# Attention into a Mish feed-forward on one core: where the seventh head pair is scaled and transposed, and four blocks of the first product computed before their Mish

## The chip, the core and the metric

One core of one Trainium2 chip runs the whole program. The engines are TensorE (PE, with its weight loads PEld), VectorE (DVE), ScalarE (ACT), GpSimd (POOL) and SyncE (SP), which here only issues DMAs. The metric is the device time of one execution in microseconds (us), lower is better. All times without a unit below are in us; places in the profile are in us from the start of the profiled span.

## The reference

Attention over 8 batches of 12 heads, 448 positions of 64 values, with one added to the softmax's sum (in the form exp(-m)), and then a feed-forward with Mish between two products.

```python
    scale = 1.0 / np.sqrt(q.shape[-1])
    scores = scale * np.matmul(q, k.transpose(0, 1, 3, 2))
    m = np.max(scores, axis=-1, keepdims=True)
    e = np.exp(scores - m)
    attn = e / (np.sum(e, axis=-1, keepdims=True) + np.exp(-m) + 1e-09)
    return np.matmul(attn, v).astype(np.float32)
...
    x = np.ascontiguousarray(attn_out.transpose(0, 2, 1, 3)).reshape(B * S, H * D)
...
    h = x @ w_in
    sp = np.where(h > 20.0, h, np.log1p(np.exp(np.minimum(h, 20.0))))
    g = h * np.tanh(sp)
    return (g @ w_out).astype(np.float32)
```

`w_in` is 768 x 2048 and `w_out` 2048 x 768. Inputs and output are float32; the kernel multiplies in bf16.

## The kernel before

The order of the instructions on every engine is written out by hand; nothing reorders them, and each engine works through its own list, waiting where data or a buffer is missing.

**Pairs, units, parts.** Two heads make a pair, six pairs a batch, 48 pairs in all. Pairs 0 to 5 are done one by one in a lead (the loop at L548). From pair 6 on three pairs make a unit, `u` = 2 to 15 (L575), and two more units finish the feed-forward. A unit has an exp part, 12 steps `n` (four per pair), and a Mish part, eight blocks `f`. In the Mish part of unit `u` the first product of the batch before is computed: units 2 and 3 do blocks 0 to 7 and 8 to 15 of batch 0. From unit 4 on the exp part also holds the second product (`w_out`) as filler.

**A pair's way.** SP loads q, k and v (`load_pair`), POOL casts them (`cast_pair`, L162 to L176), PE transposes q and k (L193), DVE and ACT copy them out of PSUM (`evac_qk`). PE computes the scores of two tiles at a time, up to three steps ahead (`scores_ahead`, three PSUM tiles `sc`), DVE takes their negated maximum (L293), ACT the exponentials with their sums (L306). `denominators` (L318) makes the reciprocals on DVE; `normalise` (L325) scales the seven tiles of `en` on DVE (L341) or POOL (L339, from a copy `rden2` of the reciprocals). The scaled tile is transposed into `eT` either by one DMA transpose on SP's queue (L345) or, for the pairs in `BY_PE`, in four parts by PE into an `mo` bank with a copy by DVE (`turn_on_pe`, L356 and L360). `av_pair` (L382) multiplies with v, and the result is cast into `xT`, the transposed input of the feed-forward (L391).

**Buffers.** There are two `mo` banks in PSUM, handed out in turn; an entry in `late` holds a copy out of one, made at the next `flush_late`. `eT` has three buffers, `en` four (`en_bufs[p % 4]`), `o_sb` four. Each DMA on SP's queue also waits until the eighth before it has landed.

**Around the change.** Unit 2 makes pairs 6, 7 and 8. At the start of its Mish part the reciprocals of all three are made at once; DVE scales pair 8 (DMA transpose), DVE scales pair 6 at block 3, and POOL scales pair 7 at block 4. Pairs 6 and 7 are turned by PE in unit 3's exp part, at the steps of `TURN_AT[1]` (L521); the value products follow at the steps of `AV_AT` (L530): pair 6 at step 5, pair 7 at 8, pair 8 at 10. The pieces of `w_in` and `w_out` are loaded by POOL's DMA queue at the steps of `W_AT` (L532) and at L629; pieces 6 to 8 of `w_in` hold blocks 8 to 11, pieces 9 to 11 blocks 12 to 15. `mm1_mish` (L399) computes one block of six matmuls, into an `mo` bank or, for block 1 of a unit, into a spare `sc` tile, and ACT applies Mish from PSUM (L412); ACT loads the table for Mish at the part's start and that for Exp at its end (L649). From pair 12 on two of three q tiles have a block-diagonal form, whose zero halves DVE writes once (L223, L224) before pairs 13 and 14.

Of the kernel before, what the change touches and what calls it, by code (L numbers as in the profile page):

```python
# [19 lines left out]
def kernel(  # L20
# [21 lines left out]
    UNITS_PER_B = HP // UNIT_PAIRS  # L42
    N_UNITS = B * UNITS_PER_B
# [157 lines left out]
    def evac_qk(p, act=False):  # L201
# [6 lines left out]
        if not is_diag(p):  # L208
            qT = qd.rearrange("d i h r -> d (i h r)")[:, 0:S]
            qkT[p] = (qT, kT)  # L210
            if act:
                nc.scalar.mul(qT, q_ps[:, 0:S], SCALE)
            else:
                nc.vector.tensor_scalar(
                    out=qT, in0=q_ps[:, 0:S], scalar1=SCALE, scalar2=None, op0=ALU.mult
                )
            if p >= DIAG_FROM:
                nc.gpsimd.tensor_copy(out=q_rest[0:64, 0, :], in_=qT[0:64, 384:S])
                nc.gpsimd.tensor_copy(out=q_rest[64:128, 1, :], in_=qT[64:128, 0:64])
        else:  # L220
            qkT[p] = (qd, kT)
            if p < DIAG_FROM + 3:
                nc.vector.memset(qd[0:64, :, 1, :], 0.0)  # L223
                nc.vector.memset(qd[64:128, :, 0, :], 0.0)  # L224
            for h in range(2):
                rows = slice(64 * h, 64 * h + 64)
                nc.vector.tensor_scalar(  # L227
                    out=qd[rows, :, h, :],
                    in0=q_ps[rows, 0:S].rearrange("d (i r) -> d i r", i=QB),
                    scalar1=SCALE, scalar2=None, op0=ALU.mult,  # L230
                )
# [66 lines left out]
    def exps(idx):  # L298
# [13 lines left out]
        if s == STEPS - 1 and p < HP:  # L312
# [11 lines left out]

    def normalise(p, dma=True, on_pool=False, shared=0):  # L325
        st = att[p]
        en = st["en"]
        if on_pool or shared:

            st["rden2"] = st_pool.tile([128, NTILE], FP32, tag="rden2", name="rden2")  # L330
            nc.vector.tensor_copy(out=st["rden2"], in_=st["rden"])  # L331
        for i in range(NTILE):
# [66 lines left out]
    def mm1_mish(b, ff):  # L399
        if ff == 0:  # L400
            gT[b] = gT_pool.tile([128, FF_T, S], BF16, tag="gT", name="gT")
        flush_late()
        spare = ff % FF_U == 1
        h_ps = sc_tiles[0][:, 0, :] if spare else mo_take()
        for dm in range(DM_T):
# [5 lines left out]
            )  # L411
        nc.scalar.activation(out=gT[b][:, ff, :], in_=h_ps[:, 0:S], func=AF.Mish)  # L412
# [80 lines left out]
    for g in range(B // 2):  # L493
# [12 lines left out]
        else:  # L506
# [9 lines left out]
    HEAD = HP  # L516

    BY_PE = (2, 4, HEAD - 1, HEAD, HEAD + 1)
    TURN_AT = (
        {0: [(4, 2)], 1: [(4, 3)], **{3 + j: [(HEAD - 1, j)] for j in range(NT)}},  # L520
        {0: [(HEAD, 0), (HEAD, 1)], 1: [(HEAD, 2)], 2: [(HEAD, 3)],  # L521
         3: [(HEAD + 1, 0)], 4: [(HEAD + 1, 1)], 5: [(HEAD + 1, 2)], 6: [(HEAD + 1, 3)]},
    )
# [6 lines left out]
    AV_AT = ({3: 4, 7: 3, 9: 5}, {5: 6, 8: 7, 10: 8})  # L530

    W_AT = ({5: 1, 9: 1}, {1: 1, 4: 1, 5: 1, 7: 1, 9: 1, 11: 1}, {3: 1, 5: 1, 7: 1, 9: 1})  # L532
# [42 lines left out]
    for u in range(UNITS_PER_B, N_UNITS + 2 * UNITS_PER_B):  # L575
# [10 lines left out]
        for n in range(steps):  # L586
# [8 lines left out]
            if u == UNITS_PER_B + 1:  # L595
                for part in TURN_AT[1].get(n, []):
                    turn_on_pe(*part)
            flush_late()
# [22 lines left out]

# [3 lines left out]
        todo = sorted(range(p0, nxt), key=lambda p: p in BY_PE)  # L625
        for f in range(FF_U):
            if moe:
                mm1_mish(b, w * FF_U + f)
            if u == UNITS_PER_B and f in (2, 6):  # L629
# [13 lines left out]
            if f == 3:  # L643
# [40 lines left out]
```

## Time and profile before

| | us |
|---|---|
| median of 3 runs (lowest to highest) | 481.56 (480.86 to 481.75) |
| the profiled execution | 479.95 |
| its span, first to last instruction | 478.0 |
| PE busy | 443.1 (93%) |
| DVE / ACT / POOL busy | 339.1 / 350.0 / 181.1 |
| mean granted TensorE clock | 0.982 |

Busy time is that in which an engine has an instruction in work; matmuls overlap, so a busy PE isn't at its peak. The granted clock is the share of full speed that TensorE was given. In a timeline row the first number is the start, the second the length, and what stands in brackets is the idle time before it and what ended it; several equal instructions are merged (x7). SPq rows are DMA issues on SP's queue; the time from issue to landing is given apart. The page's costliest groups (line, engine, operation, count, busy time and mean ns of one, idle time before) include:

```profile
L306 ACT ACTIVATE en<-sc,negm 128x448 bf16<-128x448 f32 x336 | 209.6, 637 | 26.4 <-DVE xT L391 10.4
L412 ACT ACTIVATE gT<-mo 128x448 bf16<-128x448 f32 x112 | 61.3, 547 | 68.2 <-PE mo L406 68.1
L339 POOL TENSOR_SCALAR en<-en,rden 128x448 bf16<-128x448 bf16 x122 | 76.4, 646 | 80.7 <-DVE rden L331 76.9
L341 DVE TENSOR_SCALAR en<-en,rden 128x448 bf16<-128x448 bf16 x214 | 58.6, 345 | 0.9
L459 DVE COPY o_sb<-mo 128x384 f32<-128x384 f32 (+1 forms) x65 | 32.2, 495 | 35.1 <-PE mo L472 34.8
```

Unit 2 runs from about 48 to 76.75, unit 3 to 104.29 (exp part to 92.17), and from unit 4 on a unit takes about 26.

### The profile page before, as it was taken

Reading aid. Unit: us, or ns where it says so; the run is one execution under the profiler, and the core shown is the slowest. Engines: PE = TensorE matmul, PEld = TensorE weight load, DVE = VectorE, ACT = ScalarE, POOL = GpSimd, SP = SyncE. Lnnn points to the kernel's source line nnn. Section 1 sums busy time; section 2 is a strip of 40 time slices with the busy share of each in tenths; the row PEclk is TensorE's granted clock in tenths of the full one; section 3 lists DMA queues with packets and bytes.
Section 4 is the critical chain, followed back from the end, with each engine's and each line's share of the span. In section 5 each row is a group of like instructions: output and inputs, shape, how many; then the busy total and the mean of one; then the engine's idle time right before and its main releaser. Section 6 shows DMA issues by size and latency. Waiting matters only on the chain.

```text
span 478.0 us, 8924 instructions
## 1 busy us (share of the span) xinstructions
PE 443.1 (93%) x3064; PEld 248.6 (52%) x3064; DVE 339.1 (71%) x680; ACT 350.0 (73%) x919; POOL 181.1 (38%) x315
## 2 busy tenths in 40 slices
PE   4565888898999999999999999999999999999997
PEld 2233544454655555555555555556555555556565
DVE  4888987968787886878687878788787869420021
ACT  5979678878787888979787878888897978412300
POOL 4877809255514334353535242433535340300000
PEclk9998798899999999999999999999999999999999
DMA  8999969999999989899999999899989595870113
GB/s 228 220 233 220 235 100 234 162 187 238 207 217 276 206 212 219 213 203 246 193 250 182 225 167 228 211 207 234 201 233 212 156 178 127 135 164 24 43 28 105
DMA packets 202381, 90.37 MB, mean 189 GB/s; under 512 B 159072, under 2 KB 198880, under 8 KB 202336
## 3 DMA queue, kind: packets, MB, share of 16 engines
q1 hardware_dynamic: 194848, 83.51, 81.3%
q0 software_dynamic: 7488, 6.29, 8.6%
q8 instruction: 24, 0.39, 0.3%
q14 instruction: 21, 0.17, 0.1%
HBM read 45.61 MB, written 11.01 MB: 118 GB/s over the span
## 4 chain that ended last, share of the span: by engine, by line
PE 76%; ACT 10%; DVE 9%; issue 2%; DMA 1%; POOL 0%; SPq 0%; DVEq 0%; ACTq 0%; POOLq 0%
PE mo L472 26%; PE mo L406 25%; ACT en L306 9%; PE sc L382 6%; DVE negm L293 6%; PE sc L266 5%; PE sc L406 4%; PE sc L193 3%; PE sc L272 2%; PE mo L356 1%; PE mo L382 1%; DVE en L341 1%; PE sc L280 1%; DVE eT L360 1%; DMA k_f<-in_k_dram 1%
## 5 line engine op out<-in xcount | busy, mean ns | idle before, releaser
L306 ACT ACTIVATE en<-sc,negm 128x448 bf16<-128x448 f32 x336 | 209.6, 637 | 26.4 <-DVE xT L391 10.4
L293 DVE TENSOR_REDUCE negm<-sc 128x2 f32<-128x896 f32 x192 | 180.7, 968 | 55.8 <-PE sc L275 26.0
L472 PE MATMUL mo<-w_out_sb,gT 128*128 128x384 bf16 (+1 forms) x912 | 142.3, 301 | 0.0
L406 PE MATMUL mo<-xT,w_in_sb 128*128 128x448 bf16 x672 | 137.7, 353 | 0.6 <-DVE xT L391 0.6
L412 ACT ACTIVATE gT<-mo 128x448 bf16<-128x448 f32 x112 | 61.3, 547 | 68.2 <-PE mo L406 68.1
L472 PEld LDWEIGHTS <-gT 128*128 128x128 bf16 x912 | 84.1, 98 | 48.2 <-issue 5.7
L339 POOL TENSOR_SCALAR en<-en,rden 128x448 bf16<-128x448 bf16 x122 | 76.4, 646 | 80.7 <-DVE rden L331 76.9
L406 PEld LDWEIGHTS <-w_in_sb 128*128 128x128 bf16 x768 | 72.9, 98 | 64.0 <-issue 3.0
L306 ACT ACTIVATION_READ_ACCUMULATOR en<-sc,negm 128x1 f32 x336 | 69.3, 206 | 0.0
L175 POOL CAST q_bf<-q_f 112x512 bf16<-112x512 f32 x47 | 29.0, 617 | 98.4 <-DMA q_f<-in_q_dram 98.0
L341 DVE TENSOR_SCALAR en<-en,rden 128x448 bf16<-128x448 bf16 x214 | 58.6, 345 | 0.9
L459 DVE COPY o_sb<-mo 128x384 f32<-128x384 f32 (+1 forms) x65 | 32.2, 495 | 35.1 <-PE mo L472 34.8
L266 PE MATMUL sc<-kT,qd 128*128 128x448 bf16 x168 | 47.7, 354 | 0.3 <-ACT en L306 0.2
L272 PE MATMUL sc<-kT,qd 64*128 64x448 bf16 x72 | 25.1, 411 | 12.7 <-ACT en L306 11.1
L382 PE MATMUL sc<-eT,v_bf 112*64 112x448 bf16 x288 | 34.1, 357 | 1.9 <-ACT en L306 1.7
L162 POOL CAST v_bf<-v_f 112x512 bf16<-112x512 f32 x48 | 29.5, 616 | 9.7 <-DMA v_f<-in_v_dram 8.8
L382 PEld LDWEIGHTS <-v_bf 112*64 112x64 bf16 x384 | 21.0, 112 | 22.8 <-issue 13.6
L176 POOL CAST k_bf<-k_f 112x512 bf16<-112x512 f32 x47 | 28.9, 616 | 7.5 <-DMA k_f<-in_k_dram 7.0
L227 DVE TENSOR_SCALAR qd<-sc 64x448 bf16<-64x448 bf16 x48 | 18.7, 389 | 11.9 <-PE sc L193 11.2
L266 PEld LDWEIGHTS <-qd 128*128 128x128 bf16 x168 | 16.3, 97 | 18.0 <-issue 9.2
L275 PE MATMUL sc<-kT,qd 64*128 64x448 bf16 x72 | 25.4, 415 | 0.0
L472 PE MATMUL mo<-w_out_sb,mid 128*128 128x384 bf16 x128 | 24.9, 326 | 0.0
(57 smaller groups left out, 340.1 us busy)
## 6 DMA issues: line engine op xcount, KB each, us to landing
q_f<-in_q_dram SPq DMA_DIRECT2D x48, 224.0 KB, 5.1
k_f<-in_k_dram SPq DMA_DIRECT2D x48, 224.0 KB, 5.4
v_f<-in_v_dram SPq DMA_DIRECT2D x48, 224.0 KB, 5.7
w_in_sb<-in_moe_w_in_dram POOLq DMA_DIRECT2D x12, 256.0 KB, 6.1
w_out_sb<-in_moe_w_out_dram POOLq DMA_DIRECT2D x8, 384.0 KB, 7.6
out_dram<-o_sb SPq DMA_DIRECT2D x7, 336.0 KB, 3.3
out_dram<-o_sb SPq DMA_DIRECT2D x8, 288.0 KB, 4.6
out_dram<-o_sb SPq DMA_DIRECT2D x8, 240.0 KB, 2.9
```

Source lines behind the costliest of these rows:

```text
L162: nc.gpsimd.tensor_copy(out=casted[p][2], in_=loaded.pop(p)[2])
L266: nc.tensor.matmul(sc[:, bk, 0:S], lhsT=qT[:, i].rearrange("d h r -> d (h r)"), rhs=kT, start=True, stop=True,)
L272: nc.tensor.matmul(sc[:, 0, 0:S], lhsT=qT[0:64, qa : qa + 128], rhs=kA, start=True, stop=True)
L293: nc.vector.tensor_reduce(out=negm, in_=sc[:, 0 : len(cols), 0:S], axis=AX.X, op=ALU.max, negate=True)
L306: nc.scalar.activation(out=st["en"][:, :, c, 0:SP_], in_=sc[:, bk, 0:S].rearrange("q (j c) -> q j c", j=NT), func=AF.Exp, bias=st["negm"][ ...
L339: nc.gpsimd.tensor_scalar(scalar2=1.0, op0=ALU.mult, op1=ALU.mult, **args)
L341: nc.vector.tensor_scalar(scalar2=None, op0=ALU.mult, **args)
L382: nc.tensor.matmul(av[h * 64 : (h + 1) * 64, 0:S], lhsT=v_bf[:, h, j * D : (j + 1) * D], rhs=e_h, start=(j == 0), stop=(j == NT - 1),)
L406: nc.tensor.matmul(h_ps[:, 0:S], lhsT=w_in_sb[:, dm, ff * 128 : (ff + 1) * 128], rhs=xT[b][:, dm, :], start=(dm == 0), stop=(dm == DM_T - 1),)
L412: nc.scalar.activation(out=gT[b][:, ff, :], in_=h_ps[:, 0:S], func=AF.Mish)
L459: nc.vector.tensor_copy(out=o_sb[:, cols], in_=st["o"][:, 0:n_cols])
L472: nc.tensor.matmul(st["o"][:, 0:n_cols], lhsT=src[:, ff, c0 : c0 + 128], rhs=w_out_sb[:, ff, cols], start=(ff == 0), stop=(ff == FF_T - 1),)
```

## The change

Pair 6 (`HEAD`) gets its reciprocals at step 3 of unit 2 and is scaled by POOL at step 7, with a DMA transpose that stands on SP's queue ahead of pair 8's; it leaves `BY_PE`, so PE no longer turns it, and ACT makes its `expm` apart. Pair 7's four turns stand at steps 1 to 4 of unit 3, and the value products of pairs 6, 8 and 7 at steps 2, 4 and 6. Two `w_in` pieces are queued at step 6 of unit 2 instead of at step 9 and block 2. Blocks 8 and 9 of batch 0's first product are computed at step 0 of unit 3, block 10 at step 8, block 11 at step 10; DVE copies each into an `o_sb` buffer, from which ACT applies Mish in unit 3's Mish part, in turn with blocks 12 to 15. The zero halves of the block-diagonal q tiles are written by POOL after unit 3's exp part. In the lead, pair 0's three DVE tiles are scaled before the reciprocals are copied for POOL.

```diff
+    HEAD = HP
...
-            if p < DIAG_FROM + 3:
-                nc.vector.memset(qd[0:64, :, 1, :], 0.0)
-                nc.vector.memset(qd[64:128, :, 0, :], 0.0)
...
-        if s == STEPS - 1 and p < HP:
+        if s == STEPS - 1 and p <= HEAD:
             nc.scalar.activation(out=st["expm"], in_=st["negm"], func=AF.Exp)
...
+    def for_pool(st):
+        st["rden2"] = st_pool.tile([128, NTILE], FP32, tag="rden2", name="rden2")
+        nc.vector.tensor_copy(out=st["rden2"], in_=st["rden"])
...
-        if on_pool or shared:
-
-            st["rden2"] = st_pool.tile([128, NTILE], FP32, tag="rden2", name="rden2")
-            nc.vector.tensor_copy(out=st["rden2"], in_=st["rden"])
-        for i in range(NTILE):
+
+        order = list(range(NTILE))
+        if shared and p == 0:
+            order = order[shared:] + order[:shared]
+        for i in order:
+            if i == 0 and (on_pool or shared) and "rden2" not in st:
+                for_pool(st)
...
+    def mm1_ahead(b, ff):
+
+        h_ps = mo_take()
+        mm1(b, ff, h_ps)
+        h_sb = o_pool.tile([128, d_model], FP32, tag="o_sb", name="o_sb")
+        h_sbs[b, ff] = h_sb
+
+        def evac():
+            nc.vector.tensor_copy(out=h_sb[:, 0:S], in_=h_ps[:, 0:S])
+            mo_free.append(h_ps)
+
+        late.append(evac)
+
+    def mm1_mish(b, ff, spare):
...
+        if (b, ff) in h_sbs:
+            nc.scalar.activation(out=gT[b][:, ff, :], in_=h_sbs.pop((b, ff))[:, 0:S], func=AF.Mish)
+            return
...
-    BY_PE = (2, 4, HEAD - 1, HEAD, HEAD + 1)
+    BY_PE = (2, 4, HEAD - 1, HEAD + 1)
...
-        {0: [(HEAD, 0), (HEAD, 1)], 1: [(HEAD, 2)], 2: [(HEAD, 3)],
-         3: [(HEAD + 1, 0)], 4: [(HEAD + 1, 1)], 5: [(HEAD + 1, 2)], 6: [(HEAD + 1, 3)]},
+        {1 + j: [(HEAD + 1, j)] for j in range(NT)},
...
-    AV_AT = ({3: 4, 7: 3, 9: 5}, {5: 6, 8: 7, 10: 8})
-
-    W_AT = ({5: 1, 9: 1}, {1: 1, 4: 1, 5: 1, 7: 1, 9: 1, 11: 1}, {3: 1, 5: 1, 7: 1, 9: 1})
+    AV_AT = ({3: 4, 7: 3, 9: 5}, {2: 6, 4: 8, 6: 7})
+    FIRST_AT = {0: (FF_U, FF_U + 1), 8: (FF_U + 2,), 10: (FF_U + 3,)}
+    SECOND = [ff for i in range(4) for ff in (FF_U + i, FF_U + 4 + i)]
+
+    W_AT = ({5: 1, 6: 2}, {1: 1, 4: 1, 5: 1, 7: 1, 9: 1, 11: 1}, {3: 1, 5: 1, 7: 1, 9: 1})
...
+                for ff in FIRST_AT.get(n, ()) if n == 0 else ():
+                    mm1_ahead(0, ff)
...
+                if u == UNITS_PER_B + 1:
+                    for ff in FIRST_AT.get(n, ()) if n else ():
+                        mm1_ahead(0, ff)
...
+            if (u, n) == (UNITS_PER_B, 3):
+                denominators(att[HEAD])
+                for_pool(att[HEAD])
+            if (u, n) == (UNITS_PER_B, 7):
+                normalise(HEAD, on_pool=True)
...
+        if u == UNITS_PER_B + 1:
+            for t_ in q_diag[1:]:
+                nc.gpsimd.memset(t_[0:64, :, 1, :], 0.0)
+                nc.gpsimd.memset(t_[64:128, :, 0, :], 0.0)
...
+        if u == UNITS_PER_B:
+            todo = [p0 + 2, None, p0 + 1]
...
-                mm1_mish(b, w * FF_U + f)
-            if u == UNITS_PER_B and f in (2, 6):
+                mm1_mish(b, SECOND[f] if u == UNITS_PER_B + 1 else w * FF_U + f, spare=f == 1)
+            if u == UNITS_PER_B and f == 6:
                 load_w(1)
...
-            if f == 3:
+            if f == 3 and todo[1]:
                 normalise(todo[1], dma=todo[1] not in BY_PE)
```

More of the change, by code (lines that the diff above doesn't have):

```diff
@@ L396, in av_pair, with mm1 @@
         del att[p], casted[p], qkT[p]
[L399 to L404, printed above, removed]
+    def mm1(b, ff, h_ps):
         for dm in range(DM_T):
@@ L411, in mm1_mish @@
             )
+    h_sbs = {}
+    def mm1_ahead(b, ff):
[8 more added lines that the diff above has]
+    def mm1_mish(b, ff, spare):
+        if ff == 0:
+            gT[b] = gT_pool.tile([128, FF_T, S], BF16, tag="gT", name="gT")
+        flush_late()
+        if (b, ff) in h_sbs:
+            nc.scalar.activation(out=gT[b][:, ff, :], in_=h_sbs.pop((b, ff))[:, 0:S], func=AF.Mish)
+            return
+        h_ps = sc_tiles[0][:, 0, :] if spare else mo_take()
+        mm1(b, ff, h_ps)
         nc.scalar.activation(out=gT[b][:, ff, :], in_=h_ps[:, 0:S], func=AF.Mish)
@@ L515 @@
     LAST_AV_AT = (0, 6, 9)
-    HEAD = HP
-    BY_PE = (2, 4, HEAD - 1, HEAD, HEAD + 1)
+    BY_PE = (2, 4, HEAD - 1, HEAD + 1)
     TURN_AT = (
         {0: [(4, 2)], 1: [(4, 3)], **{3 + j: [(HEAD - 1, j)] for j in range(NT)}},
-        {0: [(HEAD, 0), (HEAD, 1)], 1: [(HEAD, 2)], 2: [(HEAD, 3)],
-         3: [(HEAD + 1, 0)], 4: [(HEAD + 1, 1)], 5: [(HEAD + 1, 2)], 6: [(HEAD + 1, 3)]},
+        {1 + j: [(HEAD + 1, j)] for j in range(NT)},
     )
```

## The prediction, made before the changed kernel was run

> **What bounds the kernel now.** I read the stage table first. The stages are the exp part (12 steps) and the Mish part (8 blocks) of unit 2 (pairs 6 to 8) and unit 3 (pairs 9 to 11), and two later exp parts for comparison. Columns: stretch, its length, busy time of PE, weight loads, DVE, ACT and POOL, then granted clock, DMA share, GB/s.
>
> ```profile
> 48.00:64.00 16.00, 12.88 (x103) 7.41 (x102) 15.75 (x29) 11.49 (x35) 9.87 (x17) 0.79 1.02 206
> 65.00:76.75 11.75, 10.96 (x85) 6.06 (x84) 8.82 (x25) 8.10 (x15) 4.54 (x8) 1.00 0.70 160
> 76.75:92.17 15.42, 11.89 (x87) 6.76 (x87) 13.22 (x19) 13.69 (x45) 9.94 (x16) 0.78 1.16 208
> 92.17:104.29 12.12, 12.12 (x86) 6.70 (x85) 8.72 (x28) 8.34 (x14) 4.64 (x9) 0.99 0.89 159
> 130.17:145.50 15.33, 15.31 (x98) 7.98 (x96) 12.53 (x18) 13.85 (x44) 3.73 (x7) 1.00 1.05 229
> ```
>
> Unit 2's exp part is DVE's (15.75 of 16.00). Unit 3's exp part is ACT's and DVE's with PE partly idle, and its Mish part is wholly PE's (12.12 of 12.12) while DVE has 3.4 and ACT 3.8 to spare. From unit 5 on PE fills the exp parts too. So PE work taken out of 92.17 to 104.29 is worth its time, and work put into 76.75 to 92.17 is cheap. Next I read the chain of waits (start, length, what) and the timeline at the ends of that Mish part.
>
> ```profile
> 88.64 2.84 PE mo L382 x16
> 91.48 1.67 PE mo L406 x6
> 93.16 1.13 PE sc L406 x6
> 94.29 0.40 PE sc L193 x8
> 94.68 2.27 PE mo L406 x12
> ...
> 100.02 2.29 PE mo L406 x12
> ```
>
> ```profile
> 102.33 0.54 ACT L412 ACTIVATE gT<-mo 128x448 bf16<-128x448 f32 x1 [0.59 <-PE mo L406]
> ...
> 102.63 2.09 DVE L293 TENSOR_REDUCE negm<-sc 128x2 f32<-128x896 f32 x2 [1.36 <-PE sc L275]
> 102.89 1.28 ACT L649 ACT_TABLE_LOAD   x1
> ...
> 104.29 0.62 ACT L306 ACTIVATE en<-sc,negm 128x448 bf16<-128x448 f32 x1
> ```
>
> The chain runs through PE alone: value products, eight blocks of 1.13 to 1.15, three pairs of transposes of 0.40. DVE waits 1.36 for PE, and the next exponential starts at 104.29.
>
> **The change, stage by stage.**
>
> *Pair 0.* DVE now scales its three tiles before it copies the reciprocals for POOL. POOL's row at 17.65 starts some 0.55 later (0.82 of DVE before a 0.17 copy), its casts of pair 4 end near 22.1 instead of 21.58, and the k transposes that need them run at 22.21. Counted 0, at most 0.3 if that margin of 0.1 fails.
>
> *Unit 2, exp part.* DVE gets three small operations after step 3's reduction (rows of this shape: L319 0.15, L323 0.20, L331 0.17), ACT one more exponential of 0.23. ACT idles 0.80 before 53.39, so its part is hidden. DVE's isn't:
>
> ```profile
> 53.76 2.07 DVE L293 TENSOR_REDUCE negm<-sc 128x2 f32<-128x896 f32 x2
> 55.75 0.61 DVE L391 CAST xT<-mo 128x448 bf16<-128x448 f32 x1
> 56.28 0.61 DVE L360 COPY eT<-mo 112x896 bf16<-112x896 bf16 x1
> ```
>
> The three stand between this reduction and the xT cast; behind the cast wait PE's transposes of pair 8 (56.41, released by xT), and DVE is full to 64. **+0.55**, all of it on the path. POOL scales pair 6 after two w_in pieces (58.18 plus 1.43): seven at 0.62 from 59.6, done at 64.0. POOL was idle there for 12.6, waiting for DVE. DVE's operations in that time read PSUM, and such rows keep their length beside a busy POOL (reduction 1.08 at 38.00). The transpose of pair 6 takes SP about 4.3 from 64.1. DMA moved 0 GB/s from 64 to 66. Behind it on SP stand the transpose of pair 8 (67.42, now near 68.4) and nine loads (71.72, now near 72.7): 1.0 later, 0.4 when the shift of 0.55 is taken off. The first is wanted at step 4 of unit 3, beyond 81, and took 7.9 to land; the casts of pair 13 ran at 79.66 with loads landed near 77. Counted 0; without that cover it is 0.4.
>
> *Unit 2, Mish part.* DVE loses the seven scalings of pair 6 (1.80 at 69.15). PE has no gap from 66.17 to 74.7, so this is worth 0; at most 1.8 if PE waited for DVE, which no row there shows. The w_in piece queued at block 2 left at about 59 anyway, because POOL ran ahead.
>
> *Unit 3, exp part.* PE loses 28 transposes, DVE four copies of 0.61. In come four blocks (24 matmuls at 0.203 each, from 2.44 for 12) and four copies of 448 columns to o_sb. For these L459 shows 0.55 for 384 and 0.35 for 192; by that slope 0.62. DVE is therefore even. Blocks 8 and 9 run from 74.97, where 14 transposes took 0.99 and PE then waited 2.16 for an exponential: 2.44 fits into 3.15. The products of pairs 6, 8, 7 move from steps 5, 10 and 8 to steps 2, 4 and 6; the first delays the reduction of step 6 by about 0.65, and the last steps win it back because two copies fewer stand before them. Blocks 10 and 11 follow the last scores (88.64) where 2.84 of value products stood. I take **0** for the stage's end. Bounds: -1.7 (ACT is busy 13.69 of 15.42; all its gaps close) and +1.3 (blocks 8 and 9 at half clock, 12 at 0.37 = 4.45 against 3.15).
>
> *Unit 3, Mish part.* From the table load at 92.17, three chains lead to the next exponential. DVE: 0.18 + 0.29 + 1.81 + 0.39 + 0.79 + 1.81 + 0.17 + 0.79 = 6.23, with small gaps 6.4, then a reduction of 1.08 and 0.1: 7.6 (four memsets of 0.24 go to POOL, which idles from 86.7 to 94.98; no row shows one of POOL on 64x448, its 128x128 took 0.20, so four cost 0.8 to 2.5, at 0.62 as its scaling of 448, and fit). ACT: table 1.28, eleven operations at a spacing of 0.43 (66.29, 66.73, 67.15, 67.56), 0.1, table 1.28, 0.30: 7.7. Four of these read SBUF, which no Mish row shows; the nearest are 0.55 from PSUM and 0.62 for the cast at L176, so 0 to 0.3 more. PE: from 88.64 six blocks at 1.2 (10.83 from 91.48 to 102.31, less three times 0.40, over eight) and three times 0.4 are 8.4, to 97.0, then Mish 0.55, table and dummy 1.6: 99.2, or 7.0 after 92.17. ACT is longest: 7.8 for 12.12, **-4.3**.
>
> *Units 4 and 5.* Compute arrives 4.3 - 0.55 = 3.75 earlier; DMA doesn't. Unit 3's three transposes start as early as before (their first scaling isn't earlier on the clock), so the loads behind them and the last w_out pieces (issued from 118.3 on, the last landing near 127.3) move by some -0.5 only, and pair 12's transpose now starts at 118.1, among them, instead of 121.87:
>
> ```profile
> 121.87 7.21 SPq L345 DMA_TRANSPOSE eT<-en  x1
> ```
>
> It took 7.2 instead of 4.3 and landed after 9.3, at 131.2, 0.95 before PE wanted it (132.15). Pairs 13 and 14 landed near 135.6 and 141.3, wanted at 137.15 and 142.08: margins 1.5 and 0.8. With 3.75 less time before the products and half of each rate while the pieces still move (8.6 on SP, then 4.3 and 4.9), they land near 128.8, 133.3 and 139, wanted at 128.4, 133.4 and 138.3. PE is full there (15.31 of 15.33), so I count **+0.7**, between 0 (overlap no worse) and 3.0 (pair 14 lands at 141.3 as before, against 138.3). From unit 6 on SP idles about 7 in each unit (167.8 to 174.6), so nothing more is lost.
>
> Sum: +0.55 - 4.3 + 0.7 = **-3.05**. The profiled execution took 479.95 (span 478.0 and 1.95 around it), so 476.9 for its like; it lies 1.6 under the median of the runs, 481.56. The forecast is made for that: **478.5**.
>
> **Rivals.**
>
> *Slow clock at the seam, 479.1.* PE ran at a granted 0.50 from 89 to 92, after 2.3 with 0.88 busy (86 to 88.3). There blocks 10 to 12 now stand, and 9.5 matmuls fit where 17.5 would: 1.6 lost, PE's chain 8.7 instead of 7.0, gain 3.4. Compute then comes 2.85 earlier and some 0.4 is taken back: -2.45. Against it: by my placing PE is some 65% busy in the 3.4 before, and it held 1.00 at 1.41 of 2.00 around 61. The Trainium skill (TensorE: Matmul & The Clock Gate, Part 1) has half rate after an idle window of about 3.4 and full rate after a busy one, on a window that runs free; the 3.5 at half rate here agree, and by that rule the seam may fall either way from run to run.
>
> *DMA takes most of it back, 480.8.* If transposes and pieces only share a full DMA, pair 14 lands at 141.3 as before and PE waits 3.0 of the 3.75. For: margins of 0.8 to 1.5 against 3.75. Against: DMA moved 4 and 9 GB/s around 136, so it wasn't full.
>
> *Slower: PE becomes the bound of unit 3's exp part, 483.1.* At half clock throughout, its work up to the last scores is 12 block matmuls at 0.37, 28 transposes at 0.14, 24 products at 0.18 and nine steps of scores at 0.55: 17.8 from 74.97, to 92.8, where 88.64 stood. Blocks 10 and 11 at half rate take 4.5, the rest 6.1 and 1.9: the exponential starts at 105.3, 1.0 later than now, 1.55 with unit 2's part; each further slow stretch adds. It decides once the stage's granted clock falls under about 0.6; it was 0.58 from 78 to 82, but 0.78 over the stage, and where PE was as busy afterwards, from 82 to 86, it had 0.99.
>
> **How the numbers follow.** Forecast 0.57 (its own range 477.2 to 479.9), slow seam 0.15, DMA 0.12, slower 0.16. A measurement can tell about 0.2%, 0.96, from no change: the first two are faster (0.72), the third the same, the last slower. The low end is the forecast with exp-part gaps closing (-1.7) and little taken back, 476.5; the upper end reaches the last rival, 483.1.
>
> **What would show it.** Right: from the table load that starts unit 3's Mish part to the next exponential 7.6 to 8.2 instead of 12.12; POOL's seven scalings of pair 6 from about 59.6; unit 2 some 0.5 longer; the 12 matmuls of blocks 8 and 9 without a gap before step 3's scores; small waits of PE for eT in unit 5. Wrong: unit 3's exp part above 16.5, a granted clock under 0.6 in it, value products of unit 4 waiting for a transpose, or pair 6's transpose later than pair 8's scaling.

## The result: slower by 0.5%, and the profile after

Twenty runs of each kernel, side by side: 483.45 after (480.18 to 486.12) and 480.74 before (479.59 to 481.78), a ratio of 1.0051 with a 95% interval of 1.0033 to 1.0068. The forecast was 478.5, its upper bound 483.1. The runs also lie wider apart, 5.9 instead of 2.2, and the longer ones mostly have the lower granted clock: the seven of 484.1 to 486.1 lie at 0.973 to 0.981, the six of 480.2 to 481.6 at 0.981 to 0.993.

The first profile after is of one of the shortest executions (480.54, span 478.7, clock 0.993). Its stage table answers to the one of the prediction, in the same columns:

```profile
48.00:65.28 17.28, 12.72 (x103) 7.67 (x102) 16.33 (x32) 11.68 (x36) 14.37 (x24) 0.84 0.92 196
...
78.03:93.03 15.00, 11.27 (x90) 5.91 (x89) 13.30 (x20) 13.48 (x45) 11.42 (x20) 1.00 1.20 213
93.03:101.12 8.09, 7.20 (x58) 4.03 (x57) 7.45 (x25) 7.91 (x14) 2.38 (x6) 1.00 0.92 124
128.25:146.31 18.06, 15.42 (x99) 8.10 (x97) 12.54 (x18) 13.88 (x44) 3.71 (x7) 1.00 1.09 219
```

Unit 3's Mish part does shrink from 12.12 to 8.09, ScalarE now its longest engine. But unit 5's exp part (last row) has grown from 15.33 to 18.06, with PE no longer full. The starts of ACT's table loads, which end the parts, give the running balance:

| table load at the end of | before | after | difference |
|---|---|---|---|
| unit 2's exp part | 64.99 | 66.28 | +1.29 |
| unit 2's Mish part | 75.34 | 76.63 | +1.29 |
| unit 3's exp part | 92.17 | 93.03 | +0.86 |
| unit 3's Mish part | 102.89 | 99.72 | -3.17 |
| unit 4's exp part | 119.44 | 116.47 | -2.97 |
| unit 4's Mish part | 128.76 | 126.85 | -1.91 |
| unit 5's exp part | 145.53 | 146.31 | +0.78 |

From there to the end the two run alike (332.5 and 332.4). The chain of waits of this profile (start, length, what) says what ends unit 5's exp part:

```profile
117.71 2.70 DVE en L345 x6
...
120.48 12.02 DMA eT<-en
132.50 0.14 issue
132.64 0.95 PE sc L386 x8
...
134.89 7.83 DMA eT<-en
142.72 0.14 issue
142.86 0.95 PE sc L386 x8
```

Pairs 12 and 14's transposes stand in the chain, where before no transpose did, and unit 4's value products wait for them. So 3.17 were won by 103 and all were gone by 146. The median, 2.7 above before, needs more than this one profile shows.

### The profile page after: what moved, and what is told of

It is laid out like the page before. It is cut to its first block, busy times and chain, and to the rows that moved or that the text cites. A ratio compares the mean times of both kernels' runs of the same rounds, so it can differ in the third digit from the quotient of the medians.

```text
span 478.7 us, 8862 instructions
## 1 busy us (share of the span) xinstructions
PE 439.7 (92%) x3036; PEld 246.2 (51%) x3036; DVE 338.1 (71%) x672; ACT 349.5 (73%) x920; POOL 187.7 (39%) x326
## 4 chain that ended last, share of the span: by engine, by line
PE 71%; DVE 11%; ACT 9%; DMA 5%; issue 2%; SPq 0%; DVEq 0%; ACTq 0%
PE mo L496 25%; PE mo L405 23%; ACT en L304 7%; DVE negm L291 6%; PE sc L386 6%; PE sc L264 5%; DMA eT<-en 4%; PE sc L405 3%; PE sc L194 3%; PE sc L270 2%; DVE en L345 2%; DVE eT L364 1%; PE mo L386 1%; PE mo L360 1%; DVE xT L395 1%
## 5 line engine op out<-in xcount | busy, mean ns | idle before, releaser
L343 POOL TENSOR_SCALAR en<-en,rden 128x448 bf16<-128x448 bf16 x129 | 80.9, 647 | 74.7 <-DVE rden L325 59.4
L436 ACT ACTIVATE gT<-mo 128x448 bf16<-128x448 f32 x108 | 59.1, 547 | 64.9 <-PE mo L405 64.7
L270 PE MATMUL sc<-kT,qd 64*128 64x448 bf16 x72 | 24.5, 398 | 14.1 <-ACT en L304 12.3
L496 PE MATMUL mo<-w_out_sb,mid 128*128 128x384 bf16 x128 | 24.9, 326 | 0.0
L273 PE MATMUL sc<-kT,qd 64*128 64x448 bf16 x72 | 24.9, 402 | 0.0
```

The costliest lines, as they stand in the source:

```text
L270: nc.tensor.matmul(sc[:, 0, 0:S], lhsT=qT[0:64, qa : qa + 128], rhs=kA, start=True, stop=True)
L343: nc.gpsimd.tensor_scalar(scalar2=1.0, op0=ALU.mult, op1=ALU.mult, **args)
L496: nc.tensor.matmul(st["o"][:, 0:n_cols], lhsT=src[:, ff, c0 : c0 + 128], rhs=w_out_sb[:, ff, cols], start=(ff == 0), stop=(ff == FF_T - 1),)
```

## The experiments

Three theories went into the first runs. A: the transposes of pairs 12 to 14 collide with the last `w_out` pieces, and this DMA work, not the computing, sets the time of unit 5. B: unit 2's three small VectorE operations cost the time. C: stretches of half clock elsewhere make the typical run longer than the first profile. Each kernel was timed beside the kernel before on the same chip; ratios are to that.

### The changed kernel again

> The changed kernel unaltered, for a second profile and more times. Its runs so far go from 480.2 to 486.1 and the slower ones have the lower mean granted clock (0.973 to 0.981, against 0.989 to 0.993 for the fastest; some 2.3 us for each 0.01). Theory A (the transposes of pairs 12 to 14 and the last w_out pieces set the time of unit 5): 483.4 again, and a profile slower than 480.5 has its extra time in unit 5's exp part, as longer waits for eT (19.46 there and more). Theory C (stretches of half clock that fall on a PE that is wanted): the same median, but the extra time of a profile of 483 or more lies in a stretch with a granted clock of 0.5, outside the waits for eT.

485.88 against 480.07, ratio 1.0084 (1.0045 to 1.0123). This profile is of a more typical run (span 484.1, clock 0.974). Its chain of waits in unit 5:

```profile
119.06 2.26 DVE en L345 x6
...
121.38 13.92 DMA eT<-en
135.30 0.14 issue
135.43 1.71 PE sc L386 x8
```

The same profile's stretches of 2 there, in the columns of the stage table:

```profile
130.00:132.00 2.00, 1.20 (x8) 0.49 (x6) 0.84 (x2) 2.00 (x7) 1.05 (x2) 1.00 1.25 126
132.00:134.00 2.00, 0.00 (x0) 0.00 (x0) 0.00 (x0) 0.95 (x4) 0.00 (x0) 1.00 1.28 174
134.00:136.00 2.00, 0.57 (x4) 0.42 (x6) 0.00 (x0) 0.00 (x0) 0.00 (x0) 0.61 1.18 234
136.00:138.00 2.00, 2.00 (x10) 0.64 (x6) 0.27 (x1) 0.00 (x0) 0.00 (x0) 0.50 1.16 218
```

Pair 12's transpose took 13.92 to land, PE stood idle for 4.2, and then ran at half clock (eight value products 1.71 instead of 0.95); in the first profile, after a wait of 2.33, the same eight took 0.95. Unit 5's exp part, from table load to table load, is 23.8, where the first profile had 19.5 and before 16.8. So A's place holds, and a part of the low clock in this longer run came after PE had waited. Another part is as C has it, outside the waits for `eT`: unit 3's Mish part, begun at half clock, took 8.33 instead of 6.69.

Unit 3's first transpose also started at 97.18 instead of 95.61. The timeline says why. VectorE at the seam (where unit 3's exp part meets its Mish part) in the first profile:

```profile
91.52 0.62 DVE L422 COPY o_sb<-mo 128x448 f32<-128x448 f32 x1
92.66 0.62 DVE L422 COPY o_sb<-mo 128x448 f32<-128x448 f32 x1 [0.51 <-PE mo L405]
...
93.73 1.81 DVE L345 TENSOR_SCALAR en<-en,rden 128x448 bf16<-128x448 bf16 x7
```

and in this one:

```profile
92.57 0.62 DVE L422 COPY o_sb<-mo 128x448 f32<-128x448 f32 x1 [1.20 <-PE mo L405]
94.23 0.62 DVE L422 COPY o_sb<-mo 128x448 f32<-128x448 f32 x1 [1.04 <-PE mo L405]
...
95.31 1.81 DVE L345 TENSOR_SCALAR en<-en,rden 128x448 bf16<-128x448 bf16 x7
```

The copies of blocks 10 and 11 stand ahead of pair 9's scaling. At full clock the two blocks take 2.44 and only the second copy waits, for 0.51; at half clock they take 4.09, both copies wait for PE, and the scaling, with the DMA transpose behind it, starts 1.6 later.

### Without the second half of w_out, after and before

```diff
-        for h in range(2):
+        for h in range(1):
             for f in range(0, FF_T, 4):
...
-                    rhs=w_out_sb[:, ff, cols],
+                    rhs=w_out_sb[:, ff, (q0 % 2) * NQ : (q0 % 2 + nq) * NQ],
```

> The changed kernel without the four w_out pieces of the second column half (the second product uses the first half's columns twice, so half of the output differs): four transfers of unit 4 are gone, all computing is the same. Theory A: the transposes of pairs 12 to 14 take 4.3 on SP and land before they are wanted, unit 5's exp part is 16.5 instead of 19.46, and the kernel is 2.5 to 3 us faster than the kernel before with the same left out (about 477 to 478). Theory C: it stays at 482 to 483.5, slower than the kernel before with the same left out by 1.5 or more, with the same spread of 5 us.

> The kernel before with the same four w_out pieces left out. Both theories: 480 to 480.7, as before, since its unit 5 has no wait for eT on the chain (PE full, 15.31 of 15.33). If it were faster by over 1 us, the pieces cost something in the kernel before too, which neither theory has.

After: 479.15 (ratio 0.9965, 0.9940 to 0.9989). Before: 478.83 (0.9960, 0.9938 to 0.9981). Taking the four pieces away takes 6.7 off the changed kernel and 1.2 off the one before, so nearly all of the difference between the two goes with them. The waits for `eT` are gone in both (pairs 12 to 14 land 6.2 to 7.1 after their issue). But the changed kernel is not the 2.5 to 3 faster that A gave: something else takes back the rest. And the pieces cost 1.2 before too, which no theory had.

The profile of the changed kernel without these pieces has unit 2's table load at 67.90, with two of the three small operations far longer than in the first profile. The next run shows the same.

### Pair 6's part alone, and the blocks alone

```diff
-    FIRST_AT = {0: (FF_U, FF_U + 1), 8: (FF_U + 2,), 10: (FF_U + 3,)}
-    SECOND = [ff for i in range(4) for ff in (FF_U + i, FF_U + 4 + i)]
+    FIRST_AT = {}
+    SECOND = [FF_U + i for i in range(FF_U)]
```

> The changed kernel with the four early blocks put back: pair 6 still scaled by GpSimd and turned by DMA, blocks 8 to 15 all computed in unit 3's Mish part in plain order. Theory A: unit 2 1.3 longer, unit 3's exp part 1.5 to 2 shorter (28 transposes and four copies fewer), its Mish part 10.7 to 12.1 as before; compute reaches unit 5 at about the time of before and DMA 0.5 later, so 480 to 481.5. Theory C with the fault in unit 2's gap: as slow and as scattered as the changed kernel plus what the early blocks had gained, 484 or more.

483.64, ratio 1.0058 (1.0031 to 1.0085): above A's 481.5. Unit 5 shows no wait. In this profile the loss is in unit 2, whose table load comes at 68.64, 3.65 later than before. This profile's timeline of VectorE there:

```profile
57.21 0.69 DVE L317 SCALAR_TENSOR_TENSOR den<-sums,expm 128x7 f32<-128x7 f32 x1
57.94 0.20 DVE L321 RECIPROCAL rden<-den 128x7 f32<-128x7 f32 x1
58.24 0.91 DVE L325 COPY rden<-rden 128x7 f32<-128x7 f32 x1
59.07 0.61 DVE L395 CAST xT<-mo 128x448 bf16<-128x448 f32 x1
```

and of POOL at the same time:

```profile
57.19 0.76 POOL L159 DMA_DIRECT2D w_in_sb<-in_moe_w_in_dram  x1
57.95 0.62 POOL L176 CAST q_bf<-q_f 112x512 bf16<-112x512 f32 x1
58.50 0.62 POOL L177 CAST k_bf<-k_f 112x512 bf16<-112x512 f32 x1
```

The denominator starts 0.02 after POOL's issue of a piece and ends with it (57.90 and 57.95, 0.69 instead of 0.15); the copy ends with the cast of k (59.15 and 59.12, 0.91 instead of 0.15 to 0.23). Behind them pair 8's transposes on PE wait 2.67 (before 1.05), and PE then runs its next scores at half clock (0.58 instead of 0.37). In the first profile, where the three stay short, that wait is 2.25 and the scores take 0.58 too, so the half clock isn't theirs alone. Of the ten profiles that have all three operations at this place five show 0.69 and 0.91 or 0.92; their table loads lie at 67.3 to 68.6. In a sixth only the copy is long (0.59, ending with a cast; table load at 67.6). Where all three stay short it is 65.6 to 66.3, and in the profiles of before and its variants 65.0 to 66.3. In the cases of 0.69 the denominator starts 0.023 to 0.026 after POOL's issue of a piece, in those of 0.15 beside such an issue 0.008 to 0.024 after it: what decides at the border isn't shown.

For the blocks alone pair 6 goes back to VectorE and TensorE:

```diff
-    BY_PE = (2, 4, HEAD - 1, HEAD + 1)
+    BY_PE = (2, 4, HEAD - 1, HEAD, HEAD + 1)
...
-        {1 + j: [(HEAD + 1, j)] for j in range(NT)},
+        {1: [(HEAD, 0)], 2: [(HEAD, 1), (HEAD, 2)], 3: [(HEAD, 3)],
+         4: [(HEAD + 1, 0)], 5: [(HEAD + 1, 1)], 6: [(HEAD + 1, 2)], 7: [(HEAD + 1, 3)]},
...
-    AV_AT = ({3: 4, 7: 3, 9: 5}, {2: 6, 4: 8, 6: 7})
+    AV_AT = ({3: 4, 7: 3, 9: 5}, {5: 6, 8: 7, 10: 8})
```

> The early blocks alone: pair 6 scaled by VectorE and turned by TensorE as in the kernel before, with four blocks of the first product still ahead of Mish. Unit 2 is as before (table at 65 to 66). Unit 3's exp part holds the 28 transposes, their four copies and the blocks, so 2 to 3 us longer than the 15.4 to 17.3 of before; its Mish part is 6.7 to 8.4 instead of 9.8 to 10.7. Theory A, by which the extra transpose of pair 6 takes the only DMA hole (64 to 68): DMA is as early as before, the last pieces and transposes collide no more than before, 480 to 481.5. If the early blocks themselves were the fault: 482.5 or more.

484.66, ratio 1.0084 (1.0065 to 1.0103). The sentence in A that pair 6's transpose, by filling the DMA's hole, makes the collision falls: the hole is open again here (0 GB/s from 64 to 68), and pair 12's transpose still takes 11.0 to land. Unit 3's exp part is 17.47, the copies again wait for PE, and the first transpose starts at 100.12. Each half of the change costs about as much alone as both together, so their costs don't add.

### Two pieces earlier, and the three operations later

```diff
-    W_AT = ({5: 1, 6: 2}, {1: 1, 4: 1, 5: 1, 7: 1, 9: 1, 11: 1}, {3: 1, 5: 1, 7: 1, 9: 1})
+    W_AT = ({5: 1, 6: 2}, {1: 1, 4: 1, 5: 1, 7: 1, 9: 1, 11: 3}, {3: 1, 5: 1})
```

> The changed kernel, only the order of the w_out pieces differs: two of the four that unit 4 issues at steps 7 and 9 are issued at step 11 of unit 3, ahead of the stretch in which DMA moved 57 GB/s or less (94 to 96). Theory A (the last pieces and pair 12's transpose collide; issued 1.65 after the last piece's call it landed 12.0 later, issued 0.5 after it 13.9, issued 3.6 after it 9.3): the last piece leaves 3 to 4 us earlier, pair 12 lands before 131, unit 5's exp part is 16.7 to 17.5 instead of 19.5 to 23.8, and the time falls to about 479 to 481 with a spread under 4. Theory B (unit 2's three operations on VectorE cost the time): nothing changes, 483.5 to 486.

479.90 (478.48 to 481.54) against 480.21, ratio 0.9991 (0.9977 to 1.0005): one line of the schedule takes the whole loss away. Pair 12's transpose starts 4.8 after the last two pieces, lands after at most 8.4, and PE doesn't wait (its timeline in this profile):

```profile
129.83 2.20 PE L496 MATMUL mo<-w_out_sb,gT 128*128 128x192 bf16 x13
131.95 0.95 PE L386 MATMUL sc<-eT,v_bf 112*64 112x448 bf16 x8
```

It is no gain over before, because the work comes back in front. The chain of waits of the same profile now has pair 9's transpose, beside which the two pieces stand:

```profile
95.11 1.81 DVE en L345 x7
96.98 7.87 DMA eT<-en
104.99 0.95 PE sc L386 x8
```

```diff
-            if (u, n) == (UNITS_PER_B, 3):
+            if (u, n) == (UNITS_PER_B, 5):
                 denominators(att[HEAD])
```

> The changed kernel, only the three small VectorE operations for pair 6 (denominator, reciprocal, copy) stand two steps later in unit 2, behind the xT cast that pair 8's transposes wait for, and where GpSimd is between its pieces and its scaling. Theory B: unit 2's Mish table is loaded at 65.3 to 65.8 instead of 66.2 to 68.6, the three take 0.15, 0.20 and 0.17 to 0.23 in every profile (0.69 and 0.91 where GpSimd held them up in two of the profiles so far), and 1 to 3 us of the kernel's time go with it: 481 to 483. Theory A: unit 2 gains the same, but unit 5's products still wait for the transposes, so the median stays within 1 us of the changed kernel's.

482.64, ratio 1.0059 (1.0034 to 1.0083). The three operations are short (0.16, 0.20, 0.17), but unit 2's table load is at 66.25, no earlier, and POOL's scaling waits for them: pair 6's transpose starts at 65.56 instead of 63.97. B's gain didn't come.

Both edits together:

> Both edits together: two pieces issued earlier, and the three VectorE operations later. If both theories hold, each for its own part: unit 2 at 65.3 to 65.8, unit 3's Mish part 6.7 to 8.4, no wait for eT over 0.5 in unit 5, and 477 to 479, faster than the kernel before. If A alone holds it is as fast as the version with the earlier pieces, within 0.7.

482.07, ratio 1.0026 (1.0009 to 1.0043), slower than the pieces alone by 2.2 where B gave a gain and A alone a difference within 0.7. Pair 6's transpose is again late (65.35 against 64.40), and the DMA behind it too: unit 2's loads start 0.65 later, the last of the five pieces issued in a row lands 1.5 later, and pair 9's transpose takes 9.1 instead of 7.9. Unit 4's exp part is 19.6 instead of 17.7. Unit 2 gained nothing for it (table load at 66.05 against 66.01). That the late transpose is the cause is read from these rows; no run isolates it.

### The line that sets the time

Put side by side, the profiles show a fixed distance. Columns: start of unit 3's first transpose, start of POOL's last two `w_out` issues, start of pair 12's transpose, and its time to landing.

| kernel | first transpose | last pieces | pair 12 | landing |
|---|---|---|---|---|
| before | 95.03 | 118.30 | 121.87 | 9.3 |
| after | 95.61 | 118.83 | 120.48 | 12.0 |
| after, again | 97.18 | 120.89 | 121.38 | 13.9 |
| pair 6 alone | 99.00 | 121.87 | 125.01 | 9.7 |
| operations later | 95.59 | 118.95 | 120.60 | 12.0 |
| blocks alone | 100.12 | 123.07 | 124.97 | 11.0 |

The last pieces leave 22.9 to 23.7 after the first transpose in all six: POOL issues them behind casts that wait for loads, which stand on SP behind unit 3's three transposes (13.2 to 13.7 on SP). What was computed in between differs, and they stay. Pair 12's transpose is computing's: it starts 26.8 after the first before, 24.2 to 24.9 in the changed kernel. The less is left between last pieces and transpose, the longer it takes: 3.6 gives 9.3, 1.65 gives 12.0, 0.5 gives 13.9. Most of what unit 3's Mish part saves in the changed kernel is spent there. Two tests of this, and two repairs:

```diff
+        DM_N = 2 if b == 0 and ff >= FF_U else DM_T
-        for dm in range(DM_T):
+        for dm in range(DM_N):
```

> The kernel before with two of six matmuls in each of blocks 8 to 15 of batch 0 (four of the six terms of these blocks are left out): TensorE loses 32 matmuls, 6 us, in unit 3's Mish part, DMA and its order are untouched, and nothing of pair 6 or of the copies is changed. Theory A: the part shrinks from 10.7 to 7 or 8, but pair 12's transpose still lands 36 to 38 after unit 3's first, and at most the slack of about 1 is gained: 479 to 480.5, with waits for eT in unit 5's exp part. The prediction's reasoning (TensorE's work in this part is worth its time): 476.5 to 477.5.

480.62 against 480.32, ratio 1.0005 (0.9980 to 1.0030). The kernel before, with 32 matmuls fewer in that part, is no faster (a gain of 1 would still be hard to tell from none; one of 3 or 4 lies outside the interval). The part shrank from 10.72 to 6.22 between its table loads (93.47 and 99.69), more than expected. Pair 12's transpose starts at 121.66, 2.2 after the last pieces, and lands 35.5 after unit 3's first one, a little under the 36 to 38. This profile's chain of waits shows the same two transposes as the changed kernel's:

```profile
121.66 10.11 DMA eT<-en
...
131.90 0.95 PE sc L382 x8
...
134.18 7.81 DMA eT<-en
```

Nothing of pair 6, of copies or of early blocks is in this kernel. That shows it: TensorE's work in unit 3's Mish part wasn't worth its time.

It doesn't show that the transposes alone take the gain back. Of the 4.50 this profile gives back 1.99 in unit 4's exp part (18.54 from table load to table load, 16.55 before), ahead of any transpose in the chain, then 0.48 in unit 4's Mish part and 0.77 in unit 5's exp part. The remaining 1.26 only makes up for a unit 2 that ended 1.31 later than in the profile before. The 1.99 are VectorE's: the first exponential waits for its maximum, and the copy into `mid`, moved forward beside POOL's casts, takes 2.08 and ends 0.29 after the last cast. Before, and then with short blocks (VectorE, ScalarE):

```profile
105.63 0.78 DVE L422 COPY mid<-gT 128x1024 bf16<-128x1024 bf16 x1
...
103.83 2.08 DVE L423 COPY mid<-gT 128x1024 bf16<-128x1024 bf16 x1
101.95 0.63 ACT L306 ACTIVATE en<-sc,negm 128x448 bf16<-128x448 f32 x1 [0.76 <-DVE negm L293]
```

In the changed kernel's first profile unit 4's exp part is hardly longer than before (16.75), and that copy takes 0.42.

The short blocks and the missing second half together:

> The kernel before with both left out: two of six matmuls in blocks 8 to 15 of batch 0, and no w_out pieces of the second half (the second product uses the first half's columns twice). The short blocks alone gained nothing (480.6 for 480.3), the missing pieces alone 1.2 to 1.4 (478.8). Theory A (the pieces, by landing ahead of pair 12's transpose, take back what unit 3's Mish part gives): here the shorter part comes through, and the two together gain far more than their sum: 475.5 to 476.8. If something else in units 4 and 5 takes it back (TensorE, VectorE, the loads): 478 to 479.

478.17 against 480.59, ratio 0.9942 (0.9922 to 0.9961). The profile, of its shortest execution (476.56), has no transpose in the chain, and unit 5's exp part ends at 142.94, against 145.74 with only the pieces left out. That isn't the more than the sum that A gave: the other profile is of one of its longer executions (479.56) and was 1.22 behind already when unit 3's Mish part began. From that point to the end of unit 5's exp part the kernel before takes 53.36, 1.00 less without the pieces, 1.26 less with short blocks, 2.58 less with both. Unit 4's exp part is 18.54 here too, so VectorE's share of the loss needs no pieces. The medians don't show it either: the short part is worth 0.18% without the pieces (0.9942 against 0.9960) and -0.05% with them, and with intervals of 0.2% the two can't be told apart. The median missed the expected 475.5 to 476.8 and lies in the range for something else taking the gain back (478 to 479).

The first repair moves pair 9's scaling ahead of block 11's copy:

```diff
+            if (u, n) == (UNITS_PER_B + 1, steps - 1):
+                denominators(att[p0]["whole"])
+                normalise(p0)
             flush_late()
...
-            if f == 0:
+            if f == 0 and u != UNITS_PER_B + 1:
                 denominators(att[p0]["whole"])
```

> The changed kernel, only VectorE's order at the end of unit 3's exp part differs: pair 9's denominators and scaling stand ahead of the copy of block 11 instead of behind it. Theory A in its sharper form (the last w_out piece leaves 24 after unit 3's first transpose starts, 23.6 to 24.4 in six profiles, and pair 12's transpose lands 12 to 14 after that, whatever the computing in between does): where block 11 ran at half clock the first transpose started 1.6 late (97.18 against 95.61), so this edit is worth 0.5 to 1.5 in the median: about 482 to 484, still with waits for eT in unit 5. If the place of the copies doesn't matter: as the changed kernel, 483.5 to 486.

480.81 (479.78 to 483.82), ratio 1.0020 (0.9996 to 1.0045), 0.3 to 0.6% under the changed kernel's two ratios, so 1.5 to 3 for the 0.5 to 1.5 expected. VectorE's timeline in its profile shows the order that was wanted:

```profile
92.78 0.62 DVE L422 COPY o_sb<-mo 128x448 f32<-128x448 f32 x1
...
94.84 1.81 DVE L345 TENSOR_SCALAR en<-en,rden 128x448 bf16<-128x448 bf16 x7
96.57 0.61 DVE L422 COPY o_sb<-mo 128x448 f32<-128x448 f32 x1
```

The first transpose starts 2.44 after unit 3's table load here; with the copy of block 11 ahead it was 2.58 in two profiles, 4.2 to 4.3 in four, and 6.18 in that of the blocks alone.

Second, this order and the two pieces at step 11 of unit 3:

> The same with two of the four last w_out pieces issued at step 11 of unit 3. Theory A: 478.5 to 479.5, as fast as or faster than the version with the pieces alone (479.9) and by a little faster than the kernel before; no wait for eT over 0.5 in unit 5; unit 4's exp part still 17 to 18, since the two pieces stand beside pair 9's transpose. If the copies' place doesn't matter: 479.9.

480.21, ratio 1.0000 (0.9975 to 1.0025), above the 478.5 to 479.5 expected. Its profile is of its longest run (483.52): five pieces issued in a row from 86.64 stand beside pair 9's transpose, which takes 10.5, and the value products in unit 4 wait 3.1 for it. The collision has moved by a unit.

Then two early blocks only, with the two pieces moved, and four blocks with one piece moved:

```diff
+    FIRST_AT = {0: (FF_U, FF_U + 1)}
+    SECOND = [FF_U + i for i in (0, 2, 1, 3, 4, 5, 6, 7)]
```

> The changed kernel with two early blocks instead of four (blocks 10 and 11 stay in the Mish part, so no copies stand ahead of pair 9's scaling), and the two w_out pieces issued at step 11 of unit 3. Theory A: unit 3's first transpose starts as early as in the changed kernel's best profile or earlier (95.0 to 95.8), the Mish part is about 9 instead of 6.7 to 8.4, and since DMA sets the time behind it nothing is lost by that: 478.5 to 479.7. If the four early blocks were worth their time: 480.5 to 482.

480.61, ratio 1.0006 (0.9985 to 1.0026). The time lies in the range for blocks that are worth their time (480.5 to 482), but beside four early blocks with the same pieces moved (0.9991 and 1.0000) the intervals overlap: no gain of blocks 10 and 11 is shown, and no loss.

```diff
+    W_AT = ({5: 1, 6: 2}, {1: 1, 4: 1, 5: 1, 7: 1, 9: 1, 11: 2}, {3: 1, 5: 1, 7: 1})
```

> The changed kernel with pair 9's scaling ahead of the copy of block 11 and one w_out piece, not two, issued earlier. Two moved pieces stood in pair 9's way (its transpose took 10.5 to land in that profile), none in pair 12's (12.1). Theory A: one piece fits the hole at 94 to 97, waits for eT of at most 1 in units 4 and 5, and 479 to 480, no slower than the versions with none (480.8) and two (480.2). If the pieces' place is only noise by now: 480.2 to 480.8.

480.88, ratio 0.9997 (0.9977 to 1.0016). Pair 12's transpose still took 10.55 with one piece fewer; no gain over the others, and not the 479 to 480 that A gave.

### What unit 2 is worth

Pair 9's scaling first, without the second half's pieces; then without the copy of pair 6's reciprocals, with the pieces as they are and with two moved:

> The changed kernel with pair 9's scaling ahead of the copy of block 11 and without the w_out pieces of the second half: what the change would be worth with neither the copies nor the pieces in its way. The kernel before without those pieces took 478.8, the changed one 479.2. Theory A: 477.3 to 478.6, so of the 4 the Mish part gives up, unit 2's three VectorE operations with the slow TensorE behind them take 2 to 3 (its table at 66.2 to 68.6 instead of 65 to 65.7). If unit 2 were harmless: under 476.5.

479.41, ratio 0.9969 (0.9955 to 0.9982), above the 477.3 to 478.6 expected and no better than the kernel before without the pieces (0.9960). With neither copies nor pieces in the way the change still gains nothing in the median. In its profile, of its shortest run (478.15), unit 2's table load is at 67.40, with the 0.69 and 0.91 again, 1.7 to 2.4 behind before; unit 5's exp part ends at 143.86, 1.88 ahead of the kernel before without the pieces. Where the typical run loses that is not shown.

```diff
                 denominators(att[HEAD])
-                for_pool(att[HEAD])
+                att[HEAD]["rden2"] = att[HEAD]["rden"]
```

> The changed kernel with pair 9's scaling ahead of the copy of block 11, and without the copy of pair 6's reciprocals for GpSimd (GpSimd reads the reciprocals themselves). In five of ten profiles in which the three operations of unit 2 stand at their first place that copy took 0.91 or 0.92 instead of 0.15 to 0.23, and the first of them 0.69. If unit 2 is what is left of the loss: its table at 65.5 to 67.0 instead of 65.6 to 68.6, and a ratio to the kernel before of 0.998 to 1.000 where the version with the copy had 1.002. If it is not: 1.002 again.

> The same with two w_out pieces issued at step 11 of unit 3. With the copy it was as fast as the kernel before (1.000). If unit 2 is what is left: 0.996 to 0.998, faster than both kernels. If it is not: 0.999 to 1.001.

481.29, ratio 1.0030 (1.0010 to 1.0049), and 479.69, ratio 0.9997 (0.9982 to 1.0013). Without the copy unit 2's table load is at 66.37 and 65.99, as early as expected, but neither ratio moved. So a delay in unit 2 is seen in the profiles, and two edits that shorten or shift it bought nothing; what it costs in the end stays open. No version that does the whole work was faster than the kernel before by more than its interval; the best, the changed kernel with two pieces earlier, equals it.

## Why the prediction was wrong, step by step

**What bounds the kernel.** "PE work taken out of 92.17 to 104.29 is worth its time" is the step that failed. The chain through that part was read rightly; that the part lies on the way to a later meeting with the DMA was seen only further down and as a small correction. The short blocks in the kernel before, 4.5 off the part and nothing off the time, contradict it. What took the 4.5 back there was VectorE in unit 4's exp part (2.0) and, up to unit 5's end, 1.2 more with two transposes in the chain; in the changed kernel it was pair 12's transpose behind the last pieces (12.0 to 13.9 to landing, 9.3 before), and moving two pieces away removes the loss (0.9991). Why the rest of the gain doesn't appear even without the pieces stays open.

**Units 4 and 5.** The term was +0.7, bounded by 3.0. From unit 3's to unit 5's end the first profile gave back 3.95 (-3.17 to +0.78) and the second 7.6 (-1.60 to +6.00). The direction was named, the size was not. The pieces and loads were to move by -0.5; they moved by +0.5 and +2.6, since the first transpose came later, not as early as before. And "half of each rate while the pieces still move" gave a landing at 128.8 that came at 132.5 and 135.3. That PE would run at half clock after such a wait, as in the second profile, wasn't counted. The margins were misread too: in the trace of the kernel before pairs 13 and 14 land 7.8 and 6.4 after their issue, at 137.0 and 139.9, so pair 13 had 0.1 to spare and pair 14 2.1, not 1.5 and 0.8. And of the 7 that SP was said to idle in each unit, 1.2 are output DMAs (at 171.73).

**Unit 3's exp part.** Counted 0, bounded by -1.7 and +1.3: -0.43 in both profiles. The blocks 8 and 9 ran without a gap at full clock, as predicted. What was missed is the queue: the copies of blocks 10 and 11 wait for PE on VectorE, and pair 9's scaling, the first transpose and so the whole DMA line stand behind them.

**Unit 3's Mish part.** -4.3 predicted, -4.03 between table loads in the first profile: right, with ScalarE its longest engine. In the second it was -2.39, at half clock from 90 to 93: the slow seam, a rival given 0.15, shows in one of two profiles of the same kernel, with 1.6 lost as it said.

**Unit 2.** +0.55 for its exp part. The table load moved by 1.29 in the first profile, 0.15 of it from the lead, and by up to 3.65 in others. The argument that VectorE's operations keep their length beside a busy POOL used rows that read PSUM; the three new ones read SBUF, and two of them are held up in five of ten profiles, the copy alone in a sixth. By the Trainium skill (SBUF — State Buffer, Who interferes with whom) VectorE, in the two-port modes that a copy can enter, and GpSimd share a pair of ports that whoever comes first holds for its whole instruction; the copy's 0.91, ending with the cast, agrees. The same section has an operation with two inputs in SBUF contend only with a GpSimd instruction that reads SBUF; here such an operation took 0.69 in six profiles and ended with GpSimd's issue of a DMA, so on this point the measurement decides (what that issue reads, no row shows).

**The rivals.** "DMA takes most of it back, 480.8" had the mechanism and the place: pair 14 wanted early and landing at 142.7. That its number is so near the first profile's 480.54 is luck: 480.8 was meant for a median, and with the 1.6 between median and profile it would be 479.2 for an execution like the profiled one. It was held to be less likely because DMA moved 4 and 9 GB/s around 136. That low rate lies behind pair 12's landing at 131.2 and says nothing on the collision. "PE becomes the bound of unit 3's exp part" ended on the right side at 483.1 and for a wrong reason: in both profiles of the changed kernel the part is shorter than before (and its terms as printed add up to 17.6, not 17.8).

**Range and chances.** The range ended at 483.1 and the median is 483.45. The losses of unit 5, the seam and unit 2 were set out as single cases, while one run can have several: the second profile has the slow seam (1.6), a first transpose that starts 1.6 later for it, and the longest wait in unit 5 with half clock behind it.

## What to carry to other kernels

Before a stage is shortened, follow its time to the next place where computing meets a transfer, and compare the gain with the slack there, and with what the other engines have left to do by then: here a stage that one engine filled, shortened by 4.5, was worth nothing in the time. A transfer's start is set by what stands ahead of it on every queue, here VectorE's copies ahead of a scaling ahead of SP's transpose, so new work belongs behind whatever starts a transfer. And one profile of a kernel whose runs spread can be its best case: take a second before explaining a median.

## What the runs showed of the hardware

- Unit 4's DMA transposes land 6.1 to 7.1 after their issue in the four profiles without the last `w_out` pieces. With them pair 12's takes 7.3 to 8.4 when it starts 4.6 to 5.2 behind the last two, and 9.3 to 13.9 when it starts 0.5 to 3.6 behind.
- Two VectorE operations on 128x7 values took 0.69 and 0.91 instead of 0.15 and 0.23, each about until a GpSimd instruction begun before or during it had ended; a start 0.008 to 0.024 after POOL's issue of a DMA stayed short, one of 0.023 to 0.026 was long. A copy of 128x1024 took 0.42, 0.78 or 2.08, the last two ending 0.29 after GpSimd's last cast.
- TensorE, idle for 4.2 in unit 5, came back at a granted 0.50 for some 6, and after 2.33 idle at 1.00; the same twelve matmuls at unit 3's seam took 2.44 in one run and 4.09 in the next.
